# Eight plain loads of a two-block kernel issued by GpSimd instead of SyncE

## Chip, cores and metric

The kernel runs on one core of one Trainium2 chip. The metric is the device time of one execution in microseconds (us), the median of several runs. The engines are TensorE (PE, with its weight loads as PEld), VectorE (DVE), ScalarE (ACT), GpSimd (POOL) and SyncE (SP).

## What is computed

Two pre-norm residual blocks over 2048 tokens of width 448, in bfloat16:

```python
h  = x + A(layernorm(x), wqkv, wo)             # attention
h2 = h + B(layernorm(h), w_in, w_sp, b_sp, w_out)   # gated MLP

# A: 16 heads of 28; token s sees the 8 tokens s, s-2, ..., s-14
logits = einsum('bhsd,bhswd->bhsw', q, kg) * 28**-0.5    # masked where s-2w < 0
o = einsum('bhsw,bhswd->bhsd', softmax(logits), vg)
return o.reshape(1, 2048, 448) @ wo

# B: w_in is 448 x 1792, w_sp is 2048 x 2048, w_out is 896 x 448
z  = gelu(x @ w_in); z1 = z[..., :896]; z2 = layernorm(z[..., 896:])
g  = einsum('ts,bsf->btf', w_sp, z2) + b_sp[None, :, None]
return (z1 * g) @ w_out
```

## The kernel before

Every step is a job with a name, an engine and a list of operations. `ORDER` (line 31) is a list of all jobs written out by hand; `pl.order()` walks it, and `sch.issue` (line 136) appends each operation to its engine's own list and works out on which semaphores it must wait. So each engine runs its jobs in the order in which they stand in `ORDER`, one after another, and an operation whose semaphore is late holds back everything behind it on that engine. `ON` (line 81) is a table from a job's name to the engine that takes it, for jobs that could run on more than one.

The stages overlap. Loads of `x` and the weights come first. The norm of `x` goes by blocks of 128 tokens: DVE takes the statistics (line 619, `st`, `mv`), POOL raises variance plus epsilon to the power -1/2 (lines 609 and 610, `rs`), DVE normalizes (line 630, `xn`), and a copy of the last 64 columns (line 503, `xn<-xn`, on POOL or DVE) fills the block to 512. For blocks 4 to 15 a DMA transpose that SP issues writes the result as `xhT` (line 517). PE makes queries and keys (`xhT,wqk`) and values (`wv,xhT`), all by line 460.

Attention goes by 17 groups of keys: PE makes logits (line 808), ACT their exponentials `E` (817), DVE multiplies by a 0/1 mask (823), PE multiplies by the values (832), DVE divides (840 and 843, `otm`), a small copy fills `otm` (503), an SP transpose makes `OTs`, and POOL, DVE or ACT spread that into `OT` (503, `OT<-OTs`). PE multiplies by `wo` (460, `wo,OT`), DVE adds the residual (773), and the second norm repeats the chain of the first, up to the transposes `hnT<-xn`.

Block B: PE makes z2 (`hnT,w_in` and `w_in,hnT`, line 460), ACT takes gelu, DVE and POOL normalize z2 (lines 897 to 906 and 609, 610). Then 28 tiles of the product with `w_sp` (lines 986 and 1007), to which DVE adds the bias `bb` and multiplies by z1 (967, 970), and last the product with `w_out` (1034 and 1055), the residual (1015) and the stores. `w_sp` is read by DMA transposes from DRAM (`wsp_la`, `wsp_lb`, `wsp_hi`) that SP issues among the other transposes.

All 113 DMAs are issued by SP: `load` (line 514) has `eng="sp"` and looks the job up in `ON`, which names no load. The plain loads (line 518) that matter here are, in SP's order: `wo`, `wo_1`, `w_in3_1` (the first 384 rows of w_o in three pieces per partition, its last 64 rows into the upper half of the partitions, and the last 64 rows of w_in likewise), `w_in2_0` and `w_in0_0` (128 x 896 each), `wo_0` (the last 64 rows of w_o into the lower half), and much later `bb` (the spatial bias copied to 128 partitions) and `w_out` (128 x 7 x 448). None of the eight waits for a semaphore.

Of the kernel before, what the change touches and what calls it, by code (L numbers as in the profile page):

```python
# [85 lines left out]
        'dve', 'oc15': 'act', 'nd1_9': 'dve', 'nd1_14': 'dve', 'nd1_12': 'dve', 'nd1_13': 'dve'}  # L86
RAW2 = [0, 1, 2, 1, 1, 1, 1, 2, 1, 2, 1, 0, 0, 1, 0, 0]
XEH = {0: 2}
WLH = [4, 4, 8, 9, 18, 1, 4, 12, 24, 4, 14, 34, 6, 22, 21, 26]
# [1045 lines left out]
```

## Time and profile before

| what | value |
|---|---|
| median of 3 runs | 240.64 us (239.42 to 242.53) |
| the profiled execution | 239.89 us, of which the span from first to last instruction is 238.2 us |
| busy, share of the span | PE 97%, DVE 61%, PEld 52%, ACT 39%, POOL 20% |
| granted PE clock | 0.999 |
| DMA | 23.20 MB, all of the program's packets on one queue |

In the views below, times are us from the start of the span; durations marked ns are nanoseconds. A row of the timeline has its start, its duration, the engine, the line, the operation, the tiles (out<-in), the shape, and how many like instructions were merged; in brackets stands how long the engine was idle before it and whose end released it. SPq marks SP's sequencer issuing a DMA: its duration is that of issuing, not of the transfer.

### The profile page before, as it was taken

How to read it: one execution, taken by the hardware profiler on the slowest of the kernel's cores; microseconds unless marked ns; L12 is line 12 of the kernel's file. 1: busy time of each engine (PE TensorE's matmuls, PEld its weight loads, DVE VectorE, ACT ScalarE, POOL GpSimd, SP SyncE). 2: the span in 40 equal slices, each digit the busy share in tenths (PEclk: the TensorE clock that was granted, in tenths of full speed). 3: DMA queues.
4: the chain of work that ended last, by engine and by line, in shares of the span. 5: the costliest groups of instructions: out<-in, count | busy, mean ns of one | idle time of the engine just before them, and what ended most of it. 6: DMA issues, size and time to landing. Idle time of an engine off the chain costs nothing.

```text
span 238.2 us, 5559 instructions
## 1 busy us (share of the span) xinstructions
PE 230.2 (97%) x2374; PEld 123.9 (52%) x2380; DVE 145.7 (61%) x331; ACT 93.8 (39%) x111; POOL 47.2 (20%) x99
## 2 busy tenths in 40 slices
PE   6897999999999999999999999999999999999995
PEld 4663444645455455555555555555555555455442
DVE  5997997999998988788950039005102700763374
ACT  1788888975978787877710000000000000000000
POOL 3461543434326340403440000000000000000000
PEclk9999999999999999999999999999999999999999
DMA  6998465747685799189999910000000000002222
GB/s 178 284 165 158 109 116 118 107 113 173 119 127 92 182 135 186 37 169 180 176 189 221 202 35 0 3 0 3 0 0 4 0 3 0 3 0 74 81 77 80
DMA packets 66233, 23.20 MB, mean 97 GB/s; under 512 B 58656, under 2 KB 65952, under 8 KB 66208
## 3 DMA queue, kind: packets, MB, share of 16 engines
q1 hardware_dynamic: 66208, 22.83, 48.0%
q8 instruction: 19, 0.31, 0.6%
q14 instruction: 6, 0.05, 0.1%
HBM read 6.72 MB, written 1.84 MB: 36 GB/s over the span
## 4 chain that ended last, share of the span: by engine, by line
PE 90%; DVE 3%; DMA 3%; SPq 2%; issue 1%; ACT 0%
PE psum L986 38%; PE psum L460 34%; PE psum L1034 7%; PE psum L832 3%; PE psum L1007 3%; PE psum L808 3%; DMA x_tm<-in_A_x_dram 3%; PE psum L1055 2%; SPq L518 2%; DVE st L619 1%; DVE qkT L503 0%; DVE E L823 0%; DVE V L503 0%; ACT z2p L503 0%; DVE srg L1015 0%
## 5 line engine op out<-in xcount | busy, mean ns | idle before, releaser
L967 DVE TENSOR_TENSOR ub<-psum,bb 128x512 bf16<-128x512 f32 x28 | 18.6, 687 | 65.7 <-PE psum L986 60.9
L986 PE MATMUL psum<-wsp_hi,z2p 64*128 64x512 bf16 x384 | 42.2, 376 | 0.0
L817 ACT ACTIVATE E<-psum 128x960 bf16<-128x960 f32 (+2 forms) x34 | 31.6, 973 | 6.2 <-PE psum L808 5.9
L986 PEld LDWEIGHTS psum<-wsp_hi,z2p 64*128 64x128 bf16 x384 | 21.7, 94 | 19.7
L986 PE MATMUL psum<-wsp_la,z2p 64*128 64x512 bf16 x224 | 26.7, 376 | 0.0
L986 PE MATMUL psum<-wsp_lb,z2p 64*128 64x512 bf16 x224 | 26.5, 376 | 0.0
L460 PE MATMUL psum<-xhT,wqk 64*128 64x512 bf16 (+2 forms) x171 | 23.5, 343 | 1.7 <-DVE st L619 1.1
L460 PE MATMUL psum<-w_in,hnT 64*128 64x448 bf16 (+1 forms) x212 | 24.9, 349 | 0.0
L460 PE MATMUL psum<-hnT,w_in 64*128 64x512 bf16 (+1 forms) x184 | 24.4, 376 | 0.4 <-ACT z2p L503 0.4
L823 DVE TENSOR_TENSOR E<-E,maskb 128x1920 bf16<-128x1920 bf16 (+2 forms) x17 | 19.8, 1175 | 1.4 <-ACT E L817 1.3
L619 DVE BATCH_NORM_STATS2 st<-x_tm 128x6 f32<-128x448 bf16 x32 | 19.1, 614 | 2.5 <-DMA x_tm<-in_A_x_dram 2.4
L610 POOL TENSOR_TENSOR rs<-rs,negh 128x2 f32<-128x2 f32 (+2 forms) x23 | 18.3, 794 | 4.5 <-DVE rs L609 2.7
L897 DVE BATCH_NORM_STATS2 st<-z2p 128x6 f32<-128x448 bf16 x32 | 18.5, 605 | 0.8 <-ACT z2p L890 0.8
L986 PEld LDWEIGHTS psum<-wsp_la,z2p 64*128 64x128 bf16 x224 | 12.7, 94 | 11.5
L986 PEld LDWEIGHTS psum<-wsp_lb,z2p 64*128 64x128 bf16 x224 | 12.7, 94 | 11.5
L460 PEld LDWEIGHTS psum<-w_in,hnT 64*128 64x128 bf16 (+1 forms) x212 | 12.0, 94 | 9.5 <-ACT z2p L893 0.2
L1034 PE MATMUL psum<-w_out,z1p 128*128 128x448 bf16 x84 | 16.1, 353 | 0.0
L935 ACT ACTIVATE z1p<-psum 128x1024 bf16<-128x1024 f32 x14 | 14.2, 1022 | 4.1 <-PE psum L460 4.1
L460 PEld LDWEIGHTS psum<-hnT,w_in 64*128 64x128 bf16 (+1 forms) x184 | 10.2, 94 | 10.4 <-issue 1.3
L460 PEld LDWEIGHTS psum<-xhT,wqk 64*128 64x128 bf16 (+1 forms) x176 | 9.7, 95 | 10.4 <-DVE st L619 1.3
L503 ACT ACTIVATE qkT<-psum 128x1024 bf16<-128x1024 f32 (+1 forms) x16 | 13.3, 867 | 4.0 <-PE psum L460 2.7
L1015 DVE TENSOR_TENSOR srg<-psum,x_tm 128x448 bf16<-128x448 f32 (+2 forms) x17 | 9.4, 592 | 8.2 <-PE psum L1034 4.1
(68 smaller groups left out, 258.7 us busy)
## 6 DMA issues: line engine op xcount, KB each, us to landing
w_in<-in_B_w_in_dram SPq DMA_DIRECT2D x8, 224.0 KB, 3.3
out_dram<-srg SPq DMA_DIRECT2D x16, 112.0 KB, 1.7
x_tm<-in_A_x_dram SPq DMA_DIRECT2D x2, 448.0 KB, 6.3
w_out<-in_B_w_out_dram SPq DMA_DIRECT2D x1, 784.0 KB, 5.8
x_tm<-in_A_x_dram SPq DMA_DIRECT2D x3, 224.0 KB, 4.7
wq<-in_A_wqkv_dram SPq DMA_DIRECT2D x3, 224.0 KB, 5.3
bb<-in_B_b_sp_dram SPq DMA_DIRECT2D x1, 512.0 KB, 3.9
wv<-in_A_wqkv_dram SPq DMA_DIRECT2D x1, 336.0 KB, 6.4
```

Of the source, the lines that this page charges most:

```text
L460: ins = e.matmul(o, w, x, start=k not in seen, stop=last, **kw)
L503: j = pl.job(name, eng, key, [(lambda e: e.activation(o(), i(), AF.Copy) if eng == "act" else e.tensor_copy(o(), i()), list(reads), list(w ...
L610: power = (lambda e: e.tensor_tensor(R, A, negh[:, 0:1].to_broadcast([128, n]), ALU.pow), [rr, r_negh], r_rs[k][m:m + n])
L619: [(lambda e: e.bn_stats(st[:, m, :], src), [rsrc], [r_st[k][m]])], dve_t(D))
L817: return e.activation(o, i, AF.Exp, scale=SCALE)
L823: return e.tensor_tensor(a, a, maskb[:, mi:mi + 1, pad:pad + nq].to_broadcast([NK, NHEAD, nq]), ALU.mult)
L897: [(lambda e, m=m, k=k: e.bn_stats(st3[:, m, k, :], z2p[:, m, D * k:D * (k + 1)]), [r_z2[m]], [r_st[2][m]])], dve_t(D))
L935: return e.activation(o, i, AF.Gelu_apprx_tanh)
L967: [(lambda e: e.tensor_tensor(ub[:, s, :], psv(tk, k), bb[:, 512 * tc:512 * tc + 512], ALU.add), [r_bb], [r_ub[s]])], dve_t(512), use=[tk] ...
L986: ins = e.matmul(psv(tk, k), z2p[h, s, 128 * fc:128 * fc + 128], wsp(s, tc)[h], start=n == 0 and s == 0, stop=n == len(lots) - 1 and s == ...
L1015: [(lambda e: e.tensor_tensor(srg[:, s, c0:c1], psv(tk, k, c1 - c0), x_tm[:, m, c0:c1], ALU.add), [r_x[m]], r_srg[2 * s + (c0 > 0):2 * s + ...
L1034: ins = e.matmul(psv(tk, k, D), z1p[h, fc, 128 * (m + k):128 * (m + k) + 128], w_out[h, fc, :], start=fc == 0 and (which == 0 or not half) ...
```

## The change

Eight entries are added to `ON`, which gives eight loads to POOL. Nothing else differs; `ORDER` is the same, so each load takes its place on POOL among the POOL jobs that stand around it in `ORDER`. Line numbers behind the table are two higher.

```diff
         'act', 'od13': 'dve', 'oc11': 'dve', 'od12': 'dve', 'nd1_4': 'dve', 'nd1_7': 'dve', 'oc12': 'dve', 'od14':
-        'dve', 'oc15': 'act', 'nd1_9': 'dve', 'nd1_14': 'dve', 'nd1_12': 'dve', 'nd1_13': 'dve'}
+        'dve', 'oc15': 'act', 'nd1_9': 'dve', 'nd1_14': 'dve', 'nd1_12': 'dve', 'nd1_13': 'dve', 'w_in3_1': 'pool',
+        'w_in2_0': 'pool', 'w_in0_0': 'pool', 'wo': 'pool', 'wo_0': 'pool', 'wo_1': 'pool', 'bb': 'pool', 'w_out':
+        'pool'}
```

On POOL, in the first norm, before (`rs` is the power of the norm, `xn<-xn` and `otm<-otm` the small copies, `maskb` the attention mask being built, `OT<-OTs` the spreading of a transposed result):

```order
L596 AFFINE_SELECT maskb<-maskb 128x128
L503 COPY xn<-xn 128x64 [waits sem_dve] x3
L596 AFFINE_SELECT maskb<-maskb 128x128 [waits sem_pool]
L503 COPY otm<-otm 128x64
L609 TENSOR_SCALAR rs_67<-mv_62 128x4 [waits sem_dve]
L610 TENSOR_TENSOR rs_67<-rs_67,negh 128x4 [waits sem_pool]
L503 COPY xn<-xn 128x64 [waits sem_dve] x2
L503 COPY OT<-OTs 128x4x128 [waits sem_q29]
```

and the same place on POOL with the change:

```order
L598 AFFINE_SELECT maskb<-maskb 128x128
L520 DMA wo<-in_A_wo_dram 128x3x448
L520 DMA wo<-in_A_wo_dram 64x448
L520 DMA w_in<-in_B_w_in_dram 64x1792
L505 COPY xn<-xn 128x64 [waits sem_dve] x3
L598 AFFINE_SELECT maskb<-maskb 128x128 [waits sem_pool]
L505 COPY otm<-otm 128x64
L520 DMA w_in<-in_B_w_in_dram 128x896 x2
L611 TENSOR_SCALAR rs_67<-mv_62 128x4 [waits sem_dve]
L612 TENSOR_TENSOR rs_67<-rs_67,negh 128x4 [waits sem_pool]
L505 COPY xn<-xn 128x64 [waits sem_dve] x2
L520 DMA wo<-in_A_wo_dram 64x448
```

Three loads now stand ahead of three small copies, two ahead of the last power of the first norm, and one ahead of the first spreading copy.

On SP, the same stretch before (`xhT<-xn` are the transposes of the first norm):

```order
L517 DMA_TRANSPOSE xhT<-xn 128x4x128 [waits sem_dve]
L518 DMA wo<-in_A_wo_dram 128x3x448
L518 DMA wo<-in_A_wo_dram 64x448
L518 DMA w_in<-in_B_w_in_dram 64x1792
L517 DMA_TRANSPOSE xhT<-xn 128x4x128 [waits sem_dve]
L517 DMA_TRANSPOSE xhT<-xn 128x4x128 [waits sem_pool,sem_dve]
L517 DMA_TRANSPOSE xhT<-xn 128x4x128
L517 DMA_TRANSPOSE xhT<-xn 128x4x128 [waits sem_pool,sem_dve]
L518 DMA w_in<-in_B_w_in_dram 128x896 x2
L517 DMA_TRANSPOSE OTs<-otm 128x4x128 [waits sem_dve]
L518 DMA wo<-in_A_wo_dram 64x448
L517 DMA_TRANSPOSE xhT<-xn 128x4x128 [waits sem_pool,sem_dve]
```

and with the change:

```order
L519 DMA_TRANSPOSE xhT<-xn 128x4x128 [waits sem_dve] x2
L519 DMA_TRANSPOSE xhT<-xn 128x4x128 [waits sem_pool,sem_dve]
L519 DMA_TRANSPOSE xhT<-xn 128x4x128
L519 DMA_TRANSPOSE xhT<-xn 128x4x128 [waits sem_pool,sem_dve]
L519 DMA_TRANSPOSE OTs<-otm 128x4x128 [waits sem_dve]
L519 DMA_TRANSPOSE xhT<-xn 128x4x128 [waits sem_pool,sem_dve]
```

Only transposes are left there, with the waits that they had. Later on POOL, the bias stands between a spreading copy and two small copies of `otm`; this is the change:

```order
L505 COPY OT<-OTs 128x4x120 [waits sem_q57]
L520 DMA bb<-in_B_b_sp_dram 128x2048
L505 COPY otm<-otm 120x64 [waits sem_dve]
L505 COPY otm<-otm 112x64 [waits sem_dve]
L505 COPY xn<-xn 128x64 [waits sem_dve]
```

Before, the bias was issued by SP just ahead of one of the `OTs<-otm` transposes. `w_out` becomes the last job of POOL, behind its last power (line 612); on SP it stood between transposes of `wsp_hi`.

## The prediction

> **What bounds the kernel now.** I read the page first: who is busy, and the chain that ended last.
>
> ```profile
> span 238.2 us, 5559 instructions
> PE 230.2 (97%) x2374; PEld 123.9 (52%) x2380; DVE 145.7 (61%) x331; ACT 93.8 (39%) x111; POOL 47.2 (20%) x99
> PE 90%; DVE 3%; DMA 3%; SPq 2%; issue 1%; ACT 0%
> ```
>
> PE is the chain. Busy averages hide stages, so next comes the table by stretches, cut where the stages change:
>
> ```profile
> core 0: us, PE busy (x) PEld busy (x) DVE busy (x) ACT busy (x) POOL busy (x), PEclk, DMA share, GB/s
> 0.00:20.00 20.00, 16.16 (x205) 10.80 (x205) 16.49 (x47) 13.00 (x20) 8.74 (x27) 1.00 0.95 196
> 20.00:82.00 62.00, 61.11 (x843) 32.61 (x850) 56.69 (x123) 50.81 (x59) 24.79 (x43) 1.00 0.67 130
> 82.00:117.00 35.00, 34.60 (x346) 19.09 (x344) 29.54 (x73) 27.29 (x32) 10.43 (x23) 1.00 0.80 144
> 117.00:207.00 90.00, 90.00 (x836) 47.02 (x832) 26.74 (x59) 2.69 (x3) 3.22 (x6) 1.00 0.24 48
> 207.00:238.20 31.20, 28.28 (x152) 14.40 (x151) 16.22 (x32) 0.00 (x0) 0.00 (x0) 0.99 0.18 59
> ```
>
> From 20 to 117 us PE is idle for 0.89 + 0.40 = 1.29 us, from 117 to 207 not at all. That is the most an earlier load could give back there. But DVE is busy for 56.69 of 62 us between 20 and 82, so whatever holds DVE up there soon reaches PE, and PE has no later idle time in which to catch up.
>
> SP's queue, at the places from which loads are taken (the first row is a far bound, used below):
>
> ```profile
> 8.87 3.50 SPq L517 DMA_TRANSPOSE wsp_la<-in_B_w_sp_dram  x1
> ...
> 18.66 1.13 SPq L518 DMA_DIRECT2D wo<-in_A_wo_dram  x2
> 19.83 0.59 SPq L518 DMA_DIRECT2D w_in<-in_B_w_in_dram  x1
> 21.35 6.15 SPq L517 DMA_TRANSPOSE xhT<-xn  x4
> 27.54 1.05 SPq L518 DMA_DIRECT2D w_in<-in_B_w_in_dram  x2
> 29.79 1.19 SPq L517 DMA_TRANSPOSE OTs<-otm  x1
> 31.02 1.08 SPq L518 DMA_DIRECT2D wo<-in_A_wo_dram  x1
> 32.20 1.23 SPq L517 DMA_TRANSPOSE xhT<-xn  x1
> ...
> 76.47 0.57 SPq L518 DMA_DIRECT2D bb<-in_B_b_sp_dram  x1
> 77.16 1.20 SPq L517 DMA_TRANSPOSE OTs<-otm  x1
> ...
> 125.25 1.41 SPq L518 DMA_DIRECT2D w_out<-in_B_w_out_dram  x1
> ```
>
> No moved load is issued before 18.66, so the first 20 us, where PE loses most, stay as they are.
>
> **What SP gains.** It loses 1.13 + 0.59 + 1.05 + 1.08 + 0.57 + 1.41 = 5.83 us of issuing. At the first two places the saving buys nothing: after 20.42 and after 28.59 SP stood waiting until 21.35 and 29.79 for what it transposes. At 31.02 the next transpose can go 1.1 us sooner, at 76.47 0.6 us, at 125.25 1.4 us. The last feeds `wsp_hi`, among 90 us in which PE never waits. The others can only shrink the 1.29 us of PE idle time; I take 0 and keep 1.29 as the bound.
>
> **What POOL pays.** POOL's rows at the places where loads now stand:
>
> ```profile
> 17.75 0.29 POOL L596 TENSOR_SCALAR_AFFINE_SELECT maskb<-maskb 128x128 bf16<-128x128 bf16 x1
> 20.46 0.34 POOL L503 COPY xn<-xn 128x64 bf16<-128x64 bf16 x1 [2.42 <-DVE xn L630]
> 23.38 0.24 POOL L503 COPY xn<-xn 128x64 bf16<-128x64 bf16 x1 [2.58 <-DVE xn L630]
> 24.35 0.24 POOL L503 COPY xn<-xn 128x64 bf16<-128x64 bf16 x1 [0.74 <-DVE xn L630]
> 24.54 1.21 POOL L596 TENSOR_SCALAR_AFFINE_SELECT maskb<-maskb 128x128 bf16<-128x128 bf16 x1
> 25.70 1.15 POOL L503 COPY otm<-otm 128x64 bf16<-128x64 bf16 x1
> 28.78 0.23 POOL L609 TENSOR_SCALAR rs<-mv 128x4 f32<-128x4 f32 x1 [1.92 <-DVE mv L621]
> 29.10 1.04 POOL L610 TENSOR_TENSOR rs<-rs,negh 128x4 f32<-128x4 f32 x1
> ...
> 31.06 0.34 POOL L503 COPY xn<-xn 128x64 bf16<-128x64 bf16 x1 [0.19 <-DVE xn L630]
> 33.26 1.63 POOL L503 COPY OT<-OTs 128x512 bf16<-128x512 bf16 x1 [1.86 <-DMA OTs<-otm]
> ...
> 74.24 1.48 POOL L503 COPY OT<-OTs 128x480 bf16<-128x480 bf16 x1 [0.49 <-DMA OTs<-otm]
> 76.47 0.24 POOL L503 COPY otm<-otm 120x64 bf16<-120x64 bf16 x1 [0.74 <-DVE otm L843]
> 77.92 0.75 POOL L503 COPY otm<-otm 112x64 bf16<-112x64 bf16 x1 [1.22 <-DVE otm L843]
> ```
>
> The brackets are the cover: POOL idles where the loads go. No row shows POOL issuing a DMA, so its price c per load is unknown. The floor is what SP takes for the same loads, 0.53 to 0.59 us in the rows above. The ceiling is the longest issue in SP's rows, the 3.50 us of a transpose at 8.87. Between them lie POOL's own operations, which take two kinds of duration:
>
> ```profile
> L596 POOL TENSOR_SCALAR_AFFINE_SELECT maskb<-maskb x8: 287/292/1212, 15.0 to 73.3; 128x128 bf16<-128x128 bf16 x8
> L503 POOL COPY OT<-OTs x12: 613/722/1628, 33.3 to 84.1; 128x480 bf16<-128x480 bf16 x8, 128x512 bf16<-128x512 bf16 x2, 128x384 bf16<-128x384 bf16 x2
> ```
>
> (min, median and max in ns). I take c = 1.2: above SP's price, since POOL has to do in instructions of its own what SP's row does in 0.55, and within the 0.72 to 1.63 us of POOL's ordinary copies. Beside the row, the Trainium skill (DMA: Bandwidth & Descriptors, section "Specifications") gives about 1 us to the first byte from GpSimd and 0.6 from SyncE. By that as c, an estimate, the sum below would be 0.07 instead of 0.47. No trace here has the GpSimd figure.
>
> Place by place, with c = 1.2:
>
> A, three loads from 18.04 (17.75 + 0.29). They take 3.6 us and end at 21.64, so the copy at 20.46 is 1.2 us late. It needs 0.34, and the next copy was released by DVE only at 23.38: all three hide up to 23.38 - 18.04 - 0.34 = 5.0 us, c = 1.67. The late copy feeds one of the four transposes at 21.35; the first of these doesn't need POOL, and a later copy, at 23.38, feeds another. Cost 0.
>
> B, two loads from 26.85 (25.70 + 1.15) to 29.25, where the power chain of line 609 started at 28.78. It is late by 2 x 1.2 - 1.93 = 0.47 us. Who waits:
>
> ```profile
> 30.17 0.40 DVE L630 TENSOR_SCALAR xn<-x_tm,mv,rs 128x448 bf16<-128x448 bf16 x1 [0.41 <-POOL rs L610]
> 32.75 0.35 PEld L808 LDWEIGHTS psum<-qkT 28*128 28x128 bf16 x16 [0.42 <-DVE otm L503]
> ```
>
> DVE already stands for 0.41 us for exactly this result, and behind it are the normalizations and the divisions of three groups, for which PE waits at 32.75. So the delay goes to PE in full: 0.47 us.
>
> C, one load from 31.40, in 1.86 us of idle time before the copy at 33.26. Even 0.47 late it ends at 33.07. Cost 0. Its data are needed here:
>
> ```profile
> 38.82 0.35 PE L460 MATMUL psum<-wo,OT 64*128 64x448 bf16 x2
> 207.12 16.00 PE psum L1034 x84
> ```
>
> (timeline, and below it the chain of waits). 5.75 us are left from 33.07 to 38.82 for its landing.
>
> D, the bias from 75.72 to 76.92: the `otm` copy at 76.47 is 0.45 late and ends at 77.16. The transpose for it was issued at 77.16, behind the bias on SP; that row is gone, so it goes at about the same time. The next copy waits for DVE until 77.92. Cost 0; without the cover on SP it would be 0.45. The bias itself is read only from 117 on.
>
> E, `w_out` behind POOL's last operation, more than 80 us before PE first reads it at 207.12. Cost 0.
>
> Sum: +0.47 us on 239.89, the profiled execution's own time (span 238.2 and 1.7 around it), is 240.36. The median of the runs is 240.64, 0.75 above the profiled one; on that scale the prediction is **241.1 us**.
>
> **The sum for other prices.** Below c = 0.97 nothing is lost. Up to 1.67 the loss is 2c - 1.93. Above that, A pushes B: the copies and the select between them take 0.34 + 0.24 + 0.24 + 1.21 + 1.15 = 3.18 us, so B begins at 18.04 + 3c + 3.18, later than 26.85 from c = 1.88 on, and the loss is 5c - 7.56: 2.4 us at 2.0, 4.8 at 2.47, 9.9 at 3.5.
>
> **Rivals.** First, on the other side, POOL is held while it issues. POOL's select goes from 0.29 to 1.21 us and its copies from 0.24 to 1.15 in the rows from 24.54 on, so something holds POOL for 0.9 us at a time while DVE is busy. If an issue of 1.2 is held twice, c = 3.0, and place B loses 7.4 us: 248.0 us. It is slower by over 2% (4.8 us) from c = 2.47. For it speaks that DVE is busy for 91% of this stretch; against it, that at A and B POOL had been idle because DVE was at statistics and normalizations, not mask products alone. The Trainium skill (SBUF — State Buffer, section "SBUF: two separate sides") says that GpSimd can't write a load's descriptors while a VectorE operation holds the port that they share, and gives 620 ns alone against 3100 beside such an operation. By that figure as c, the estimate is 5 x 3.1 - 7.56 = 7.9 us lost, 248.5. The trace shows the holding for POOL's copies and selects, not for a DMA.
>
> Second, held once: c = 2.0, and the loss is 2.4 us: 243.0, inside 2%.
>
> Third, the shorter SP queue gives back PE's idle time, all of it: 240.64 - 1.29 = 239.35. For it speaks that transposes behind the loads at 31.02 and 76.47 go sooner. Against it: POOL's results gate the same transposes.
>
> Fourth, the change does less than it says: POOL issues at SP's 0.55 us, everything hides in POOL's idle time, and SP's saving hides too: 240.6, unchanged.
>
> **How the numbers follow.** The forecast has 0.50, the fourth 0.13, the third 0.10, held once 0.15, held twice 0.12. Over 2% (about what a measurement of this kernel can tell from no change) faster needs 4.8 us, where PE's idle time offers 1.29: 0.01. Slower by over 2% is held twice, 0.12. The rest, 0.87, is no change. The range goes from the third rival, 239.3, to 5 us above the forecast, 246.0 (c about 2.6), and leaves out most of the 0.12 above.
>
> **What would show it.** In the changed kernel's profile: eight DMA issues on POOL of about 1.2 us; the power of line 612 near 29.6 instead of 29.10; the idle time of DVE before line 632 near 30.6 risen from 0.41 to about 0.9; PE's idle time between 20 and 82 risen from 0.89 to about 1.4; and from 82 on every stretch as long as before. The prediction is wrong if an issue takes over 1.9 us at A or B, so that DVE waits for `rs` by microseconds, or if the span shrinks by more than 1.3 us, which would mean that PE's work was being slowed by something that its idle time doesn't show.

## The result and the profile after

| | median | range | executions |
|---|---|---|---|
| kernel before | 241.69 us | 238.94 to 242.75 | 20 |
| changed kernel | 243.76 us | 240.74 to 249.28 | 20 |

The ratio of the times is 1.0083, with a 95% interval of [1.0055, 1.0111]. That is no change at 2%, as forecast, but it is a loss of about 2.0 us that the interval separates from zero, and it did not arise where the forecast had put its 0.47 us. The ratio leaves out executions more than 1.5% above the fastest of the same kernel, here six of the changed kernel's 20, from 244.40 us up.

The profiled execution of the changed kernel took 241.6 us, 1.7 more than the profiled one of before. The page of the profile has these lines on the span, the engines and the chain that ended last:

```profile
span 239.9 us, 5559 instructions
PE 229.7 (96%) x2374; PEld 115.1 (48%) x2380; DVE 145.3 (61%) x331; ACT 93.6 (39%) x111; POOL 50.8 (21%) x107
PE 80%; DMA 7%; DVE 6%; POOL 2%; ACT 2%; issue 1%; SPq 1%; POOLq 0%; DVEq 0%; ACTq 0%
```

DMA has risen from 3% to 7% of the chain, while POOL's sequencer, which now issues the eight loads, holds 0% of it (POOLq). The table by stretches, with the columns as in the prediction (from 20 us on):

```profile
20.00:82.00 62.00, 58.72 (x823) 31.10 (x828) 55.88 (x122) 50.45 (x58) 25.36 (x48) 1.00 0.72 130
82.00:117.00 35.00, 34.95 (x352) 17.57 (x350) 27.73 (x68) 26.59 (x31) 9.46 (x21) 1.00 0.72 130
117.00:207.00 90.00, 90.00 (x838) 40.59 (x836) 27.04 (x60) 3.54 (x4) 5.20 (x9) 1.00 0.27 52
```

PE's idle time from 20 to 82 us went from 0.89 to 3.28 us, that from 82 to 117 from 0.40 to 0.05. What POOL pays for the loads stands in its timeline:

```profile
17.58 1.58 POOL L520 DMA_DIRECT2D wo<-in_A_wo_dram  x2
19.14 0.54 POOL L520 DMA_DIRECT2D w_in<-in_B_w_in_dram  x1
...
26.27 1.11 POOL L520 DMA_DIRECT2D w_in<-in_B_w_in_dram  x2
28.25 0.23 POOL L611 TENSOR_SCALAR rs<-mv 128x4 f32<-128x4 f32 x1 [0.87 <-DVE mv L623]
...
30.81 0.61 POOL L520 DMA_DIRECT2D wo<-in_A_wo_dram  x1
...
75.56 0.62 POOL L520 DMA_DIRECT2D bb<-in_B_b_sp_dram  x1
...
124.75 1.09 POOL L520 DMA_DIRECT2D w_out<-in_B_w_out_dram  x1
```

A load costs POOL 0.54 to 0.62 us here, and more only where it has three or seven pieces per partition. After the two loads at 26.27 POOL still stood idle for 0.87 us until DVE released the power of line 611. So nothing was lost in issuing. The loss is in PE's timeline. Of before:

```profile
22.65 1.46 PE L460 MATMUL psum<-xhT,wqk 128*128 128x512 bf16 x6
...
31.04 1.78 PE L460 MATMUL psum<-xhT,wqk 128*128 128x512 bf16 x9 [0.16 <-issue]
...
78.79 0.92 PE L460 MATMUL psum<-w_in,hnT 64*128 64x448 bf16 x8
...
82.75 1.04 PE L460 MATMUL psum<-hnT,w_in 64*128 64x512 bf16 x8 [0.40 <-ACT z2p L503]
```

and of the changed kernel, the same four groups of matmuls:

```profile
22.12 1.46 PE L462 MATMUL psum<-xhT,wqk 128*128 128x512 bf16 x6
...
31.19 1.78 PE L462 MATMUL psum<-xhT,wqk 128*128 128x512 bf16 x9 [0.84 <-DMA xhT<-xn]
...
80.84 0.93 PE L462 MATMUL psum<-w_in,hnT 64*128 64x448 bf16 x8 [1.97 <-DMA hnT<-xn]
...
84.24 0.61 PE L462 MATMUL psum<-hnT,w_in 64*128 64x512 bf16 x4
```

PE is 0.53 us ahead at 22 us, loses that and 0.15 more around a wait for a transpose `xhT` at 31 us, and is 2.05 us late at 80.84, after a wait of 1.97 us for a transpose `hnT`. At 84.24 it is only 1.49 us late, since the wait of before at that place, 0.40 us in its row, is gone; the span ends 1.7 us later. Both waits are for transposes that SP issued at the usual time. How long these were in flight is shown by the DMA view (KB each, median us from issue to landing), for a window around one issue at a time. In the kernel before, `xhT` issued at 26.29 and `hnT` issued at 74.32:

```profile
xhT<-xn SPq DMA_TRANSPOSE x1, 2.5
...
hnT<-xn SPq DMA_TRANSPOSE x1, 3.4
```

In the changed kernel, the same transposes issued at 26.15 and 74.23, and the bias that POOL issued at 75.56:

```profile
xhT<-xn SPq DMA_TRANSPOSE x1, 4.7
...
bb<-in_B_b_sp_dram POOLq DMA_DIRECT2D x1, 512.0 KB, 5.2
hnT<-xn SPq DMA_TRANSPOSE x1, 6.5
```

`hnT` landed at 74.23 + 6.5 = 80.7 instead of 74.32 + 3.4 = 77.7. In between, from 77.5 to 78.5, the queues of the changed kernel moved (packets, MB, time taken as a share of 16 engines):

```profile
q0 software_dynamic: 57, 0.23, 115.5%
q1 hardware_dynamic: 2, 0.00, 0.1%
```

q0 is POOL's queue and carries the bias; q1 is SP's and carries the transposes, and in that microsecond it all but stood still. From 76.5 to 77.5, though, q1 had moved 496 packets, against 577 in the kernel before, so the bulk of the transpose had most likely gone, and what came late was its rest. The Trainium skill (DMA: Bandwidth & Descriptors, "Queues, rings and completion order") says that each DMA engine takes turns between its queues, packet by packet. By that, if the packets of this view are those packets, q1 would have moved about as many as q0 as long as it had work queued; how much it had is not shown, so the 2 beside 57 neither bear the rule out nor refute it.

### The profile page after: what moved, and what is told of

Its sections match the earlier page's. It is cut to its first block, busy times and chain, and to the rows that moved or that the text cites. A ratio compares the mean times of both kernels' runs of the same rounds, so it can differ in the third digit from the quotient of the medians.

```text
span 239.9 us, 5559 instructions
## 1 busy us (share of the span) xinstructions
PE 229.7 (96%) x2374; PEld 115.1 (48%) x2380; DVE 145.3 (61%) x331; ACT 93.6 (39%) x111; POOL 50.8 (21%) x107
## 4 chain that ended last, share of the span: by engine, by line
PE 80%; DMA 7%; DVE 6%; POOL 2%; ACT 2%; issue 1%; SPq 1%; POOLq 0%; DVEq 0%; ACTq 0%
PE psum L988 37%; PE psum L462 25%; PE psum L1036 7%; DMA xhT<-xn 3%; PE psum L1009 3%; DMA hnT<-xn 3%; PE psum L810 2%; PE psum L1057 2%; PE psum L834 2%; PE psum L705 1%; DVE E L825 1%; POOL rs L612 1%; DMA wq<-in_A_wqkv_dram 1%; DVE st L621 1%; DVE xn L632 1%
## 5 line engine op out<-in xcount | busy, mean ns | idle before, releaser
L988 PEld LDWEIGHTS psum<-wsp_hi,z2p 64*128 64x128 bf16 x384 | 18.7, 94 | 22.8
L988 PEld LDWEIGHTS psum<-wsp_lb,z2p 64*128 64x128 bf16 x224 | 10.9, 94 | 13.3
L988 PEld LDWEIGHTS psum<-wsp_la,z2p 64*128 64x128 bf16 x224 | 10.9, 94 | 13.3
L462 PEld LDWEIGHTS psum<-w_in,hnT 64*128 64x128 bf16 (+1 forms) x212 | 11.0, 94 | 12.8 <-DVE st L621 2.4
L462 PEld LDWEIGHTS psum<-hnT,w_in 64*128 64x128 bf16 (+1 forms) x184 | 9.4, 94 | 10.7 <-issue 0.5
```

Of the source, the lines that this page charges most:

```text
L462: ins = e.matmul(o, w, x, start=k not in seen, stop=last, **kw)
L988: ins = e.matmul(psv(tk, k), z2p[h, s, 128 * fc:128 * fc + 128], wsp(s, tc)[h], start=n == 0 and s == 0, stop=n == len(lots) - 1 and s == ...
```

## The experiments

The theory after this reading: a plain load on a queue of its own holds up the transposes that SP has in flight, and the bias, which meets a transpose that PE is about to need, is the whole loss. The main rivals: the loss is spread over the eight loads; it hangs on the kind of queue; or it hangs on the bytes that go first. All ratios are against the kernel before on the same chip. The traces, one execution of each kernel, differ by up to about 2 us by the time the first norm ends (the `xhT` matmuls at 31.04 above start at 33.02 in e1), so ratios carry the verdicts, and the traces show where waits are, not totals. In the expectations, the fifth xn transpose is the `hnT` of 74.32, the sixth is the next `hnT`, and the twelfth x transpose is the `xhT` of 26.29.

| kernel | ratio | 95% interval |
|---|---|---|
| e1, all but the bias on POOL | 0.9965 | [0.9938, 0.9993] |
| e2, the bias alone on POOL | 1.0072 | [1.0046, 1.0098] |
| e3, all eight, the bias beside `w_out` | 0.9972 | [0.9937, 1.0007] |
| e4, the bias alone, on ACT | 1.0015 | [0.9988, 1.0043] |
| e5, half of the bias early, half late | 1.0051 | [1.0023, 1.0079] |
| e6, the bias on SP, ahead of `hnT` | 1.0014 | [0.9982, 1.0045] |
| e7, bias on SP, two loads later on POOL | 0.9981 | [0.9950, 1.0012] |
| e8, bias and these two on SP | 1.0002 | [0.9971, 1.0032] |
| e9, all eight, the bias 12.5 us earlier | 1.0104 | [1.0041, 1.0166] |
| e10, these two alone on POOL | 0.9965 | [0.9933, 0.9996] |
| e11, all eight, the bias three jobs later | 1.0103 | [1.0052, 1.0155] |
| e12, six, bias and `w_out` on SP | 0.9992 | [0.9957, 1.0028] |

**Which of the eight.** e1 takes the changed kernel and puts the bias back:

```diff
+ON['bb'] = 'sp'
```

> The bias goes back to SP, the other seven loads stay on POOL. Theory 1 (the bias, on a queue of its own, is served ahead of the hnT transpose that SP queued before it, and PE waits 2.0 us for that transpose): the transpose issued near 74.3 lands within 3.6 us again, PE has no wait for hnT, ratio to the kernel before 0.998 to 1.002. Theory 2 (the seven other loads, or POOL's time for issuing, carry the loss): the ratio stays near 1.008. Theory 3 (half and half: the wait for xhT near 31 counts as much): 1.003 to 1.005.

e2 takes the kernel before and moves the bias alone:

```diff
+ON['bb'] = 'pool'
```

> The kernel before with the bias alone on POOL. Theory 1: the hnT transpose lands some 6.5 us after its issue, PE waits 1.5 to 2.2 us for it near 79, ratio 1.006 to 1.009. Theory 2: no loss, 0.999 to 1.001. Theory 3: 1.003 to 1.005.

e1 took 240.87 us against 241.89, e2 243.85: the loss goes with the bias and comes with it. e1's transpose, issued at 76.29 in its execution, flew as before:

```profile
hnT<-xn SPq DMA_TRANSPOSE x1, 3.4
```

e2's flight of the same transpose, with the bias on POOL:

```profile
hnT<-xn SPq DMA_TRANSPOSE x1, 6.4
```

and e2's list of PE's waits (total, times, longest) begins with it:

```profile
PE psum L462 <- DMA hnT<-xn: 1.9, 1, 1.9
```

**When the bias goes.** In e3 all eight stay on POOL, but the bias goes out just ahead of `w_out`:

```diff
+ORDER.remove(691)
+ORDER.insert(ORDER.index(708), 691)
```

> All eight loads on POOL as in the change, but the bias last but one, ahead of w_out and behind POOL's last power, near 124. Theory 1: the hnT transposes land as before, PE waits for none of them, and DVE's first add, near 138, finds the bias landed by about 130: ratio 0.997 to 1.001. Theory 2 (POOL's issuing as such): unchanged at 1.008. What could go wrong: the transposes of wsp_lb and wsp_hi behind the two loads land up to 5 us late, which PE reaches only after 135.

e3 took 241.63 us against 241.89: with the bias on POOL but away from the exposed transpose, the one that PE waited for, the loss is gone. So the engine that issues it is not what costs.

e11 moves it by three of POOL's jobs, behind the copy that ended at 78.77, so that it meets the next `hnT`:

```diff
+ORDER.remove(691)
+ORDER.insert(ORDER.index(374) + 1, 691)
```

> The changed kernel with the bias's load moved on GpSimd by three instructions, from 75.56 us to behind the xn copy that ended at 78.77 us, when the data of the fifth xn transpose has landed in a kernel without the hold. Theory (it holds whichever transpose is in flight): the fifth xn transpose lands 3.4 to 3.6 us after its issue and its matmuls do not wait, and instead the sixth one (hnT, issued at 78.84, 3.3 to 3.4 us in flight so far) lands after 5 to 6.5 us; its matmuls came 0.25 us too early in the kernel before, so they wait 1.5 to 3 us; time 1.005 to 1.012 of the kernel before. Rival (only the fifth one is exposed, for instance because it is the one that shares its flight with another transpose): time 0.996 to 1.001.

The theory held in the main. The fifth `hnT` landed after 3.9 us, a little more than expected, and nothing waited for it; the sixth, issued at 81.61 in this execution, took 5.2 us (3.3 in the kernel before):

```profile
hnT<-xn SPq DMA_TRANSPOSE x1, 5.2
```

and PE waited for that one:

```profile
86.90 1.04 PE L466 MATMUL psum<-hnT,w_in 64*128 64x512 bf16 x8 [2.21 <-DMA hnT<-xn]
```

e9 moves it the other way, to a place where POOL has nothing to do and no `hnT` that I thought exposed is in flight:

```diff
+ORDER.remove(691)
+ORDER.insert(ORDER.index(40) + 1, 691)
```

> The changed kernel with all eight loads on GpSimd, but with the bias's load moved there from 75.56 us to behind the mask at 63.24 us, where GpSimd had nothing to do until 69. Theory (the harm of the bias is that it meets the fifth xn transpose, which the matmuls take 1.0 us after it lands; the engine that issues it is free): the fifth xn transpose lands 3.4 to 3.6 us after its issue, no wait behind it; the transposes in flight from 63 to 69 us land up to 3 us later, which their users are taken to bear; time 0.996 to 1.002 of the kernel before. Rival (a 512 KB load on GpSimd's queue costs the matmuls its 2 us wherever transposes are in flight): time 1.006 to 1.010, with the wait before 75 us.

Here the theory's choice of place failed and the rival was right: 1.0104, from six executions with a median of 243.79 us against 241.97. The bias was issued at 63.04, and the transposes issued at 62.39 (`hnT`) and 65.14 (`OTs`) flew for

```profile
hnT<-xn SPq DMA_TRANSPOSE x1, 5.8
...
OTs<-otm SPq DMA_TRANSPOSE x1, 7.1
```

against 3.7 and 4.1 us in the kernel before. The late `OTs` held up DVE, which spreads it into `OT`. DVE's list of waits (total, times, longest) has a line that it does not have in the kernel before:

```profile
DVE OT L509 <- DMA OTs<-otm: 1.1, 1, 1.1
```

That wait ended at 72.30, the mask product for the next group followed it on DVE, and the attention groups ran late into PE:

```profile
73.83 0.96 PE L838 MATMUL psum<-V,E 128*128 128x29 bf16 x32 [0.62 <-DVE E L829]
...
78.28 0.56 PE L838 MATMUL psum<-V,E 128*128 128x29 bf16 x16 [1.04 <-DVE otm L849]
```

The rows name DVE, which was itself late. So the fifth `hnT` is not special: three places between 63 and 82 us cost 0.7 to 1.0% each by their ratios (e11's, like e9's, rests on six executions, with a median of 243.56 us), and of the places tried for the whole bias on POOL only the late one (e3) was free.

**Bytes, order or queue.** e5 sends the first half of the bias from the changed kernel's place and the second half behind `w_out`:

```diff
-        load("bb", lambda: bb[:], lambda: B_b_sp.rearrange("(o n) -> o n", o=1).to_broadcast([128, S_TOK]), [r_bb], 0.6, (1.4, 2.1), key=28.0,
+        load("bb", lambda: bb[:, 0:1024], lambda: B_b_sp[0:1024].rearrange("(o n) -> o n", o=1).to_broadcast([128, 1024]), [r_bb], 0.6, (1.4, 2.1), key=28.0,
...
+        j_wout.ops.append((lambda e: e.dma_start(bb[:, 1024:2048], B_b_sp[1024:2048].rearrange("(o n) -> o n", o=1)
+                                                 .to_broadcast([128, 1024])), [], [r_bb2], True))
...
-                     [r_bb], [r_ub[s]])], dve_t(512), use=[tk], rel=(tk, k, 1))
+                     [r_bb if tc < 2 else r_bb2], [r_ub[s]])], dve_t(512), use=[tk], rel=(tk, k, 1))
```

> The changed kernel with the bias's load cut in two: its first half (256 KB) goes out from GpSimd at the same place as before, the second half right behind w_out's load. Nothing is left out. Theory (the bias's packets, running from a queue of their own, hold up the transpose in flight for as long as they run): the hold is halved, so the fifth xn transpose (hnT) takes about 4.9 us from issue to landing, between 3.44 (kernel before) and 6.48 (changed kernel); the matmuls behind it wait about 0.5 us instead of 1.97; time about 1.001 of the kernel before (0.998 to 1.003). Rival (the hold has a fixed length, whatever the bytes): landing after 6.3 to 6.5 us, a wait of 1.8 to 2.0 us, time 1.006 to 1.010.

```profile
hnT<-xn SPq DMA_TRANSPOSE x1, 6.0
```

The wait in its list:

```profile
PE psum L463 <- DMA hnT<-xn: 1.5, 1, 1.5
```

Half the bytes took only 0.5 of the 3.1 us off the delay (6.0 against 6.5, with 3.4 undisturbed), and the ratio is 1.0051. That is much nearer to the rival's fixed length than to the theory, whose statement that the hold lasts as long as the bias's bytes run does not fit this run. What makes the rest of it is open.

e6 keeps the bias on SP, but ahead of the fifth `hnT`:

```diff
+ORDER.remove(691)
+ORDER.insert(ORDER.index(337), 691)
```

> The kernel before, with the bias's load moved on SyncE from just behind the fifth xn transpose to just ahead of it: one queue, the bias's bytes first. Theory (the harm is in two queues running side by side; within one queue the transpose only waits for the bytes ahead of it): the transpose is issued about 0.6 us later and lands about 1.0 to 1.5 us later than in the kernel before; the matmuls wait 0 to 0.5 us; time 1.000 to 1.002 of the kernel before. Rival (it does not matter which queue the bias is in, only that its 512 KB come first): landing about 3 us later as in the changed kernel, a wait of 1.8 to 2.0 us, time 1.006 to 1.010.

SP's timeline and the flight:

```profile
75.09 0.58 SPq L522 DMA_DIRECT2D bb<-in_B_b_sp_dram  x1
75.81 1.74 SPq L521 DMA_TRANSPOSE hnT<-xn  x1
```

```profile
hnT<-xn SPq DMA_TRANSPOSE x1, 4.8
```

```profile
PE psum L464 <- DMA hnT<-xn: 1.0, 1, 1.0
```

The flight is 1.4 us longer, and the issue itself came later by the bias's 0.6 us; PE waited 1.0 us, between the two expectations, and the ratio can't be told from 1. In this execution the bias, ahead of the transpose in one queue, cost it part of what it costs from another queue. Behind it, as in the kernel before, PE did not wait for the transpose.

e4 gives the bias to ACT, whose queue is of the same hardware kind as SP's:

```diff
+ON['bb'] = 'act'
```

> The kernel before with the bias alone issued by ScalarE at the same place in the order. Theory 1a (any second queue lets the bias overtake the transpose): the hnT transpose lands 5.5 us or more after its issue and PE waits 1 to 3 us, ratio 1.004 to 1.012. Theory 1b (it is peculiar to the queue of GpSimd, whose packets are made by software): the transpose lands within 4 us, PE does not wait for hnT, and only about 0.6 us of ScalarE's time is added, ratio 0.999 to 1.003.

The interval reaches from no loss to 0.43%, over half of e2's, and the median of all twelve executions, 243.00 us, is 1.11 us above the kernel before's. The profiled execution, at 244.10 us among the slowest of its twelve, has

```profile
hnT<-xn SPq DMA_TRANSPOSE x1, 6.3
```

```profile
82.62 0.93 PE L462 MATMUL psum<-w_in,hnT 64*128 64x448 bf16 x8 [1.80 <-DVE otm L845]
```

The row names a DVE operation, but the transpose, issued at 76.19, landed at 82.5, just before these matmuls, which read it. So the same delay can come with a hardware queue. But from 79.75 to 80.5 of this flight the trace has no packet of any queue starting, so the bias's bytes are not all of it; how often it happens, and how much of it the bias makes, stays open.

**The other seven.** The two `w_in` pieces issued at 26.27 held up a transpose `xhT` (4.7 us instead of 2.5). e7, on the changed kernel, takes the bias back to SP and moves these two on POOL into idle time some 13 us later:

```diff
+ON['bb'] = 'sp'
+for job in (22, 18):
+    ORDER.remove(job)
+    ORDER.insert(ORDER.index(261) + 1, job)
```

> The changed kernel with the bias's load back on SyncE, and with two of the six weight loads (the w_in pieces issued at 26.27 to 27.38 us) moved on GpSimd to behind its copy that ended at 37.95 us, where GpSimd had nothing to do until 44. Theory (those two loads held up the twelfth x transpose, 4.68 us in flight instead of 2.46, which cost the lead of about 0.5 us that the earlier loads on GpSimd had won): the transpose lands after about 2.5 us, no wait at the matmuls of that piece, and the time is 0.993 to 0.996 of the kernel before, a little under the 0.9965 of the run with the bias alone put back. Rival (the lead is lost anyway at a later wait): 0.996 to 0.999.

e8 takes them and the bias back to SP:

```diff
+ON.update(dict.fromkeys(('bb', 'w_in2_0', 'w_in0_0'), 'sp'))
```

> The changed kernel with three of its eight loads back on SyncE: the bias, and the two w_in pieces that GpSimd issued at 26.27 to 27.38 us. Theory (these three are all that the change costs; the other five are free or bring a lead of about 0.5 us before 21 us): the twelfth x transpose lands about 2.5 us after its issue, the fifth xn transpose about 3.4 us, no wait at either, time 0.993 to 0.997 of the kernel before. Rival (the 0.35% that the run with the bias alone put back was faster came from SyncE's time saved by the two w_in pieces as well): 0.997 to 1.000.

e10 moves these two alone, in the kernel before:

```diff
+ON.update(dict.fromkeys(('w_in2_0', 'w_in0_0'), 'pool'))
```

> The kernel before with only the two w_in pieces issued at 27.54 to 28.59 us on SyncE moved to GpSimd, at the place where the changed kernel has them (26.27 to 27.38 us). Theory (they hold up the twelfth x transpose, but its user comes late enough when nothing else has won a lead): that transpose lands 4.0 to 4.7 us after its issue instead of 2.46, a wait of 0 to 0.3 us at its matmuls, the later statistics of GpSimd unchanged; time 0.998 to 1.002 of the kernel before. Rival (the prediction's place B at its upper price, or a full hold of 2 us on the way of the matmuls): 1.004 to 1.010.

e12, on the changed kernel, takes the bias and `w_out` back to SP:

```diff
+ON.update(dict.fromkeys(('bb', 'w_out'), 'sp'))
```

> The changed kernel with the bias and w_out back on SyncE, so that only the six weight loads before 32 us are on GpSimd. Theory (the six are free or bring up to 0.3%, and w_out's place at 125 us costs nothing, since the matmuls have work until its neighbours land): no wait at the fifth xn transpose, PE without a gap from 117 to 207 us as in every kernel so far, time 0.995 to 1.000 of the kernel before, the same within the interval as with w_out on GpSimd (0.9965). Rival (w_out on GpSimd had cost something that the other gain hid): 0.990 to 0.994.

The mechanism shows again: with the two on POOL at their place (e10) this transpose, issued at 28.16, flew for 3.7 us, and in e7 and e8 for 2.5. The row of e10:

```profile
xhT<-xn SPq DMA_TRANSPOSE x1, 3.7
```

In e10 it costs nothing, because its matmuls came late enough; PE has no wait there beyond the 0.16 us that the kernel before had too:

```profile
32.91 1.78 PE L463 MATMUL psum<-xhT,wqk 128*128 128x512 bf16 x9 [0.16 <-issue]
```

It is not free in every execution. PE's lists of waits (total, times, longest) have this transpose in e12 and in e3, the two rows in that order:

```profile
PE psum L465 <- DMA xhT<-xn: 0.8, 1, 0.8
...
PE psum L465 <- DMA xhT<-xn: 3.1, 1, 3.1
```

The second is of e3's profiled execution, at 244.80 us the slowest of its twelve, where the transpose flew for 6.7 us.

The theories behind e7 and e8, that avoiding this hold keeps a lead of 0.5 us, fell: 0.9981 and 1.0002 are no better than e1's 0.9965. e12 at 0.9992 says the same of `w_out` within its interval: putting it back on SP brought nothing. The five kernels that leave the bias on SP and move some of the other seven (e1, e7, e8, e10, e12) lie between 0.9965 and 1.0002, and their intervals overlap. So by the ratios the seven cost nothing that can be told from noise, and bring at most a few tenths of a per cent, although the two `w_in` pieces can make PE wait. e1 and e10 are the fastest, just clear of 1 by their own intervals; with e8 and e12 beside them I don't call either a gain that is settled.

## Why the prediction was right, and where its steps failed

- **The verdict and the time** held: no change at 2%, and 243.76 us lies inside the range, 2.7 above the forecast. That is luck: the upper part of the range was drawn for a dear issue on POOL, c up to about 2.6 us, and the loss came from somewhere else.
- **Term B, +0.47 us, the whole sum, was mis-sized.** It took 1.2 us for a load on POOL; one-piece loads took 0.54 to 0.62. With that, place B loses nothing, as the prediction's own formula has it below 0.97, and POOL's idle time of 0.87 us before line 611 confirms it. The fourth rival, that POOL issues at SP's price, was right on this point. The Trainium skill (SBUF — State Buffer, "SBUF: two separate sides") gives 3100 ns beside a VectorE operation that holds the port; the eight issues here, with DVE busy for 55.88 of the 62 us around four of them, show nothing of the kind: they took 0.54 to 1.09 us each, by the rows above.
- **Places A, C and E at zero** held. e12 and PE's unbroken 90.00 us from 117 to 207 bear E out.
- **Term D, the bias at zero, was the step that failed.** It followed the copies on POOL and the `OTs` transpose that was queued behind the bias on SP. It did not ask which transfers were already in flight, and neither did term B, whose two loads held up an `xhT`. On SP the bias was issued at 76.47, behind the `hnT` of 74.32, and its bytes ran behind that transpose's bytes. On POOL it was issued only 0.9 us sooner, at 75.56, and its packets ran before that transpose had landed, which it did 3.0 us later than before. This term measured +1.7 us by e2 (0.0072 x 241.89), against the 0.45 that the prediction gave as its worst case.
- **What SP gains, 0**, held within the intervals; in e1, where the bias stays on SP, 5.83 - 0.57 = 5.26 us less of issuing on SP bought at most 0.35%.
- **The signs named in advance** were half right: PE's idle time from 20 to 82 did rise, to 3.28 instead of 1.4, but through `hnT` (1.97 us) and `xhT` (0.84) and not through `rs`; DVE's idle time before line 632 stayed at 0.41 us.
- **The rivals** all priced issuing or SP's queue. None had the load's data compete with a transfer of another queue, and that is what happened.

## What to carry to other kernels

When a load moves to another engine's queue, list the transfers that will be in flight while it runs, and when the first user of each arrives. Here a place behind an urgent transfer in the same queue had protected that transfer at no cost. Issuing a plain load cost the idle GpSimd about as much as it had cost SyncE (0.54 to 0.62 us against 0.53 to 0.59); what cost time was the moment at which its data ran.

## What the runs showed of the hardware

- A 512 KB load on another queue made a transpose in flight land 1.9 to 3.1 us late, at three places (the changed kernel's, e9's and e11's), and POOL's queue got 57 of 59 packets in the microsecond that is shown. Halving the load took only 0.5 us off. Each of these is one execution.
- A wait of PE can be followed by a lower granted clock, and so cost more than its length. In e11 the granted clock (the column after POOL's) fell about 1 us after the wait of 2.21 us had ended:

```profile
87.00:88.00 1.00, 1.00 (x12) 0.51 (x11) 1.00 (x4) 0.00 (x0) 0.69 (x1) 0.99 0.92 167
88.00:89.00 1.00, 1.00 (x8) 0.46 (x6) 1.00 (x5) 0.00 (x0) 0.03 (x1) 0.50 2.09 108
...
90.00:91.00 1.00, 1.00 (x8) 0.44 (x6) 0.84 (x2) 0.40 (x1) 0.28 (x2) 0.50 1.12 227
91.00:92.00 1.00, 1.00 (x11) 0.54 (x9) 0.38 (x2) 1.00 (x2) 0.23 (x1) 0.81 0.80 180
```

  Three microseconds at 0.50 and one at 0.81 are about 1.7 us of work lost on top of the wait. After the wait of 1.97 us in the changed kernel the clock stayed at 1.00 in that stretch; in e3's profiled execution it stood at 0.50 from 35 to 38 us, after the wait of 3.1 us for `xhT`, which ended at 34.53. The Trainium skill (TensorE: Matmul & The Clock Gate, "Part 1: The HAM clock gate") has the clock halved after an idle window of about 3.4 us; in this trace 2.21 us came before it.
